# A shorter float64 decoding, and five blocks of w_out decoded piece by piece inside the first output tile

## The chip, the cores and the metric

One core of one Trainium2 chip runs the whole program. The metric is the device time of one execution in microseconds (us); lower is better. Five engines work side by side, each through its own list of instructions in order: PE (TensorE, matmuls), DVE (VectorE), ACT (ScalarE), POOL (GpSimd) and SP (SyncE), which here issues every DMA.

## The reference, cut to what matters

Three layers follow one another: a delta-rule attention over 768 steps (4 batches, 8 heads of 48), a soft mixture of experts over 32 slots ("slot MLP" below), and a two-layer MLP over all 3072 tokens. The last two are what the change touches:

```python
def _moe_ref(x, phi, w1, w2):
    ...
    for e in range(E):
        h = np.maximum(slot_input[e] @ w1[e], 0.0)
        slot_out[e] = h @ w2[e]
    ...
    return (c @ slot_out).astype(np.float32)

def _moe2_ref(x, w_in, w_out):
    h = x @ w_in                     # 3072x384 @ 384x2048
    g = np.maximum(0.01 * h, h)
    return (g @ w_out).astype(np.float32)   # 2048x384
```

`w_in` and `w_out` arrive as float64, all other arrays as float32.

## The kernel before, in words

**Stages.** Attention runs in 24 steps (`for s in range(NST)`, L658), each over 32 of the 768 positions, up to about 322 us. The slot MLP (L829 to L913) streams the 32 tiles of `w1` and `w2` (768 KB each, `load_w`, L556) through whatever SBUF slots are free and ends at about 377 us. The token MLP (L961 to L987) fills the rest: six tiles `B` of 512 tokens, each over 16 slices `ft` of the 2048 hidden features.

**The token MLP.** Since `x` is `c @ slot_out`, the kernel multiplies `slot_out` with `w_in` first: `make_G` (L924) computes 256 columns of that product with nine matmuls into one PSUM tile `gpsum`, ACT takes one part of it (`gh`, L935) and DVE writes `Gs` (L936). There are eight such sets, made during the first tile. For each slice: one matmul `hps` (L975), ACT copies it (`hs`, L980), DVE takes the maximum of h and 0.01 h (`gf`, L981), ACT rounds it to float16 (`gh`, L982), POOL forms the remainder (`gl`, L983). `down` (L938) then runs 12 matmuls into `ops` for the previous slice: eight with `gh`, four with `gl`. `hps` has two PSUM buffers, so the matmul of slice n+2 waits for the maximum of slice n. `gpsum` has one.

**Float64 decoding.** PE wants float16 pairs, so each 128x768 block of `w_in` and `w_out` (eight of each, 768 KB as float64) is decoded. `from_f64` (L508) works on the 32-bit words `hi` and `lo` with four DVE instructions: L513 and L514 build a float32 `top` from sign, exponent and upper mantissa of `hi`; L516 takes its power of two; L517 multiplies `lo` with that, which gives the rest `m`. Then ACT rounds 1024 `top` to float16 (L530 for `w_in`, L805 for `w_out`), and two more DVE instructions (L532 and L533, or L806 and L807) form the second float16. That is six DVE instructions and one ACT instruction per block.

**Where the blocks are decoded.** `w_in` blocks 0 to 4 are decoded during the last attention steps, 5 to 7 at the head of the slot MLP. `w_out` block q is loaded by `load_wo(q)` (L793, two buffers `raw64`) and decoded by `conv_wo(q)` (L798): blocks 0 to 3 inside the loop over the groups of the slot MLP (L889 to L896), blocks 4 to 7 at the slices 0 to 3 of the first token tile (L969 to L973), each as one piece. In the loop over groups `make_cT` (L814) also transposes the routing weights; DVE copies each transposed group from PSUM into `cT` (L825).

**What sets the order.** The text of the program does not fix an engine's list. The framework simulates a timeline and orders each engine by priority; `tc.high_priority` shifts a priority, `tc.issue_after(x)` keeps an instruction behind x. On the chip each list is then run strictly in order. A DMA list entry waits until the eighth DMA before it has landed, so SP has at most eight loads on their way, and an entry that waits for a buffer holds up all behind it.

Of the kernel before, what the change touches and what calls it, by code (L numbers as in the profile page):

```python
# [41 lines left out]
def drain(gen):  # L42
    for _ in gen:
        pass
# [3 lines left out]
def fused_kernel(ctx: ExitStack, tc: tile.TileContext, kq, kv, bu, phi, w1, w2, wi, wo, out):  # L48
# [458 lines left out]

    def from_f64(raw, m, top, scale):  # L508


        hi, lo = raw[:, :, 1], raw[:, :, 0]
        mf = m.bitcast(F32)
        ve.tensor_scalar(m, hi, 0x07FFFFFF, 3, ALU.bitwise_and, ALU.logical_shift_left)  # L513
        ve.scalar_tensor_tensor(top.bitcast(U32), hi, 0xC0000000, m, ALU.bitwise_and, ALU.bitwise_or)  # L514
        yield
        ve.tensor_scalar(m, top.bitcast(U32), 0xFF800000, None, ALU.bitwise_and)  # L516
        ve.scalar_tensor_tensor(mf, lo, scale, mf, MULT, MULT)  # L517
        yield
# [7 lines left out]
    def conv_wi(q):  # L526
        t = W[0, q] = place(3 * q, [128, 2, 768], F16)
        m, top = place(30, [128, 768], F32), place(33, [128, 768], F32)
        yield from from_f64(raw64.pop(q), m.bitcast(U32), top, 2.0 ** -42)
        sc.activation(t[:, 0], top, AF.Copy, scale=1024.0)  # L530
        yield
        ve.scalar_tensor_tensor(top, top, 1024.0, t[:, 0], MULT, SUB)  # L532
        ve.tensor_tensor(t[:, 1], top, m, ADD)  # L533
        yield
# [258 lines left out]
    def load_wo(q):  # L793
        raw = p_c.tile([128, 768, 2], U32, tag="raw64", name="raw64")
        sy.dma_start(raw.rearrange("p n w -> p (n w)"), wo[q].bitcast(U32))
        raw64[q] = raw

    def conv_wo(q):  # L798
        if q % 2 == 0:
            pair[0] = late([128, 2, 2, 768], F16, q // 2)  # L800
        t = W[1, q] = [pair[0][:, q % 2, i] for i in range(2)]
        m = p_c.tile([128, 768], U32, tag="m", name="m")
        top = p_c.tile([128, 768], F32, tag="top", name="top")
        drain(from_f64(raw64.pop(q), m, top, 2.0 ** -42))
        sc.activation(t[0], top, AF.Copy, scale=1024.0)  # L805
        ve.scalar_tensor_tensor(top, top, 1024.0, t[0], MULT, SUB)  # L806
        ve.tensor_tensor(t[1], top, m.bitcast(F32), ADD)  # L807

# [5 lines left out]
    def make_cT(g):  # L814
# [7 lines left out]
        for k in range(4):  # L822
            pe.transpose(tp[:, k, :], cs[:, k].rearrange("p a b c -> p (a b c)"), id16)

        ve.tensor_copy(cT[:, 512 * g:512 * g + 512].rearrange("p (k i b) -> p k b i", k=4, b=4),  # L825
                       tp.rearrange("p k (b i) -> p k b i", b=4))

# [40 lines left out]
    def convert(q):  # L868
        with tc.high_priority(offset=-500):
            conv_wo(q)  # L870

# [7 lines left out]
    for g in range(4):  # L879
# [9 lines left out]
        elif g < 3:  # L889
            if g == 1:  # L890
                free.extend([4, 5])
            convert(g - 1)
            load_wo(g + 1)
        else:
            convert(2)
            convert(3)  # L896
    with tc.high_priority(offset=CHAIN_PRIO):
# [40 lines left out]
    def down(B, ft, gh, gl, ops):  # L938
# [12 lines left out]
        for t in range(4):  # L951
# [7 lines left out]
            sy.dma_start(oT[4 * B + t], ob)  # L959

    Gs = p_os.tile([128, 2048], F16, name="Gs", bufs=1)  # L961
    with tc.high_priority(offset=CHAIN_PRIO):
        g_ins = make_G(0)
    for B in range(6):
        ops = [ps_o.tile([128, 384], F32, tag="o", name="ops") for _ in range(4)]
        for ft in range(16):
            if B == 0 and ft % 2 == 0 and ft < 14:
                make_G(ft // 2 + 1)
            if B == 0 and ft < 4:  # L969
                with tc.issue_after(last_w[0]):  # L970
                    load_wo(4 + ft)
                with tc.issue_after(g_ins):
                    convert(4 + ft)  # L973
            hps = ps_h.tile([128, 512], F32, tag="h", name="hps")
# [5 lines left out]
            sc.activation(hs, hps, AF.Copy, scale=2.0 ** -12)  # L980
            ve.scalar_tensor_tensor(gf, hps, 0.01 * 2.0 ** -12, hs, MULT, MAX)  # L981
            sc.activation(gh, gf, AF.Copy)  # L982
# [47 lines left out]
```

## Time and profile before

| what | us |
|---|---|
| median of 3 runs (lowest, highest) | 607.33 (603.05, 607.85) |
| the profiled execution, its own time | 609.56 |
| its span in the profile | 607.8 |
| DVE busy in the span | 410.2 |
| PE busy in the span | 515.0 |

The span is what the profiler saw from the first instruction to the last; 1.8 us of the execution lie around it. Views count from the start of the span. A row of a timeline that holds several instructions (x2) gives the time from the first start to the last end, so the distance between starts tells the pace better than the duration.

### The profile page before, as it was taken

How to read it: one execution, taken by the hardware profiler on the slowest of the kernel's cores; microseconds unless marked ns; L12 is line 12 of the kernel's file. 1: busy time of each engine (PE TensorE's matmuls, PEld its weight loads, DVE VectorE, ACT ScalarE, POOL GpSimd, SP SyncE). 2: the span in 40 equal slices, each digit the busy share in tenths (PEclk: the TensorE clock that was granted, in tenths of full speed). 3: DMA queues.
4: the chain of work that ended last, by engine and by line, in shares of the span. 5: the costliest groups of instructions: out<-in, count | busy, mean ns of one | idle time of the engine just before them, and what ended most of it. 6: DMA issues, size and time to landing. Idle time of an engine off the chain costs nothing.

```text
span 607.8 us, 20075 instructions
## 1 busy us (share of the span) xinstructions
PE 515.0 (85%) x8368; PEld 376.3 (62%) x8368; DVE 410.2 (67%) x1082; ACT 291.1 (48%) x696; POOL 207.6 (34%) x217
## 2 busy tenths in 40 slices
PE   7706888989989998976867677789999999999996
PEld 5605877978878988866752222456555555555553
DVE  3899988999779889997668966994424242333331
ACT  1313555546545666564432212545656565555552
POOL 9504212311331332431101000345554545454542
PEclk9655999999989999898966878999999999999999
DMA  9965775775966757769899996300101000010101
GB/s 237 252 131 108 150 173 123 171 192 102 215 139 139 170 121 191 181 177 252 209 398 416 415 414 249 104 1 2 52 1 53 0 29 25 2 53 1 53 0 53
DMA packets 71194, 87.37 MB, mean 144 GB/s; under 512 B 42944, under 2 KB 59584, under 8 KB 71104
## 3 DMA queue, kind: packets, MB, share of 16 engines
q1 hardware_dynamic: 71104, 86.09, 50.9%
q8 instruction: 66, 1.08, 0.8%
q14 instruction: 24, 0.20, 0.1%
HBM read 70.53 MB, written 4.72 MB: 124 GB/s over the span
## 4 chain that ended last, share of the span: by engine, by line
PE 61%; DVE 19%; DMA 11%; issue 4%; ACT 3%; SPq 1%; DVEq 0%; ACTq 0%
PE ops L943 28%; PE gm L189 6%; DMA arena<-in_w_dram 6%; PE sps L420 6%; PE hps L975 3%; PE ksu L377 3%; PE y L430 3%; PE ksu L369 2%; PE ksu L399 2%; DVE arena L283 2%; DMA kqb<-in_kq_dram 2%; PE y L385 2%; DVE arena L269 1%; DVE arena L287 1%; DVE arena L229 1%
## 5 line engine op out<-in xcount | busy, mean ns | idle before, releaser
L983 POOL TENSOR_TENSOR gl<-gf,gh 128x512 f16<-128x512 f32 x96 | 112.6, 1189 | 162.2 <-ACT gh L982 90.0
L943 PE MATMUL ops<-late,gh 128*128 128x384 f16 x768 | 143.6, 326 | 0.3 <-ACT gh L982 0.3
L981 DVE SCALAR_TENSOR_TENSOR gf<-hps,hs 128x512 f32<-128x512 f32 x96 | 62.3, 686 | 112.8 <-ACT hs L980 107.8
L943 PEld LDWEIGHTS <-gh 128*128 128x128 f16 x768 | 75.0, 98 | 56.7 <-ACT gh L982 3.0
L943 PE MATMUL ops<-late,gl 128*128 128x384 f16 x384 | 81.2, 326 | 0.2 <-POOL gl L983 0.2
L980 ACT ACTIVATE hs<-hps 128x512 f32<-128x512 f32 x96 | 52.5, 594 | 52.4 <-PE hps L975 52.4
L982 ACT ACTIVATE gh<-gf 128x512 f16<-128x512 f32 x96 | 60.4, 630 | 32.9 <-DVE gf L981 27.6
L327 POOL TENSOR_TENSOR vs<-kv,nn 128x384 f32<-128x384 f32 x24 | 20.4, 849 | 137.0 <-DMA kv<-in_kv_dram 90.1
L420 PE MATMUL sps<-u,khb 128*128 128x48 f16 x1104 | 55.0, 195 | 8.8 <-ACT u L404 2.8
L189 PE MATMUL gm<-kqr,arena 128*64 128x64 f32 x640 | 46.0, 311 | 18.6 <-DVE mm L205 18.6
L420 PEld LDWEIGHTS <-khb 128*128 128x128 f16 x1104 | 51.3, 117 | 13.9 <-issue 10.1
L283 DVE TENSOR_TENSOR arena<-arena 128x81 f32<-128x81 f32 (+12 forms) x150 | 55.4, 369 | 0.1
L189 PEld LDWEIGHTS gm<-kqr,arena 128*64 128x64 f32 x640 | 42.4, 222 | 20.7 <-DVE mm L205 18.9
L943 PEld LDWEIGHTS <-gl 128*128 128x128 f16 x384 | 37.4, 98 | 25.2 <-POOL gl L983 0.8
L269 DVE SCALAR_TENSOR_TENSOR arena<-arena 128x28 f32<-128x28 f32 (+27 forms) x186 | 51.9, 289 | 0.3
L287 DVE TENSOR_TENSOR arena<-arena 128x81 f32<-128x81 f32 (+12 forms) x150 | 51.1, 341 | 0.0
L399 PE MATMUL ksu<-z,tmb 128*128 128x48 f16 x576 | 27.4, 194 | 12.9 <-DMA tmb<-tc 5.5
L404 ACT ACTIVATE u<-ksu 128x192 f16<-128x192 f32 x48 | 15.7, 329 | 44.9 <-PE ksu L399 41.7
L430 PE MATMUL y<-u,tmb 128*128 128x48 f16 x576 | 35.2, 196 | 1.3 <-issue 1.3
L385 PE MATMUL y<-st,kqb 128*32 128x48 f32 x1472 | 29.2, 230 | 5.9 <-issue 5.9
L377 PE MATMUL ksu<-st,kqb 128*32 128x48 f32 x1472 | 33.1, 233 | 1.3 <-issue 0.7
L399 PEld LDWEIGHTS <-tmb 128*128 128x128 f16 x576 | 24.3, 118 | 15.8 <-issue 12.1
(167 smaller groups left out, 888.0 us busy)
## 6 DMA issues: line engine op xcount, KB each, us to landing
we<-in_w_dram SPq DMA_DIRECT2D x22, 768.0 KB, 12.4
kv<-in_kv_dram SPq DMA_DIRECT2D x24, 384.0 KB, 4.8
kqb<-in_kq_dram SPq DMA_DIRECT2D x46, 192.0 KB, 5.2
kqr<-in_kq_dram SPq DMA_DIRECT2D x20, 384.0 KB, 6.5
arena<-in_w_dram SPq DMA_DIRECT2D x10, 768.0 KB, 10.8
tmb<-tc SPq DMA_DIRECT2D x96, 64.0 KB, 3.4
arena<-in_wi_dram SPq DMA_DIRECT2D x8, 768.0 KB, 8.2
raw<-in_wo_dram SPq DMA_DIRECT2D x8, 768.0 KB, 14.1
```

The costliest lines, as they stand in the source:

```text
L189: end["gm"] = pe.matmul(gm[64 * bp:64 * bp + 64, h, :], kb[:, k, bp, :, h], c[:, k, bp, :, :, h], start=(h == 0), stop=True, skip_group_ch ...
L269: ve.scalar_tensor_tensor(R[:, i, 0:j], R[:, j, 0:j], gu[:, i, j:j + 1], R[:, i, 0:j], MULT, ADD)
L283: ve.tensor_tensor(tv, gu[:, j + 2:, j:j + 1].to_broadcast([128, n, w]), R[:, j:j + 1, 0:w].to_broadcast([128, n, w]), MULT)
L287: ve.tensor_tensor(R[:, j + 2:, 0:w], R[:, j + 2:, 0:w], tv, ADD)
L399: last_u[A] = pe.matmul(ksu[A][:, 256 + 48 * hh:304 + 48 * hh], tmb[s % 2][:, a, A, :, hh], z[:, b, 48 * hh:48 * hh + 48], start=False, st ...
L420: last_s[0] = pe.matmul(sps[A][:, bp, hh, :], kb[:, a, A, bp, :, hh], u[:, b, hh, :], start=False, stop=(s == NST - 2 and i == 2), skip_gr ...
L430: end["mu"] = pe.matmul(y[:, 4 * A + hh, :], mv[:, a, A, :, hh], u[:, b, hh, :], start=(s == 0 and A == 0 and hh == 0 and i == 0), stop=(i ...
L943: pe.matmul(ops[t], g[:, 128 * t:128 * t + 128], w, start=(ft == 0 and i == 0), stop=(ft == 15 and i == 2))
L980: sc.activation(hs, hps, AF.Copy, scale=2.0 ** -12)
L981: ve.scalar_tensor_tensor(gf, hps, 0.01 * 2.0 ** -12, hs, MULT, MAX)
L982: sc.activation(gh, gf, AF.Copy)
L983: gp.tensor_tensor(gl, gf, gh, SUB)
```

## The change

The decoding drops the rest `m`: a third DVE instruction shifts `lo` right by 29 bits and puts its three upper bits under the mantissa of `top`. The second float16 comes from `top` alone. That is four DVE instructions per block (new L510, L511, L513 and L528 or L800), and the float32 it passes through is the float64 cut at 23 mantissa bits. The two blocks of `w_in` in flight no longer share one `top`. `raw64` gets a third buffer. The copy into `cT` goes from DVE to ACT (new L819). Block 3 of `w_out` leaves the slot MLP; blocks 3 to 7 become a generator, `late_wo`, of three pieces each, and each slice of the first tile draws one piece (the first slice two) behind its maximum. Blocks 4 and 5 are requested right behind the last `w2` tile, 6 and 7 when the buffers of 3 and 4 have been read.

```diff
-    def from_f64(raw, m, top, scale):
-        hi, lo = raw[:, :, 1], raw[:, :, 0]
-        mf = m.bitcast(F32)
-        ve.tensor_scalar(m, hi, 0x07FFFFFF, 3, ALU.bitwise_and, ALU.logical_shift_left)
-        ve.scalar_tensor_tensor(top.bitcast(U32), hi, 0xC0000000, m, ALU.bitwise_and, ALU.bitwise_or)
-        yield
-        ve.tensor_scalar(m, top.bitcast(U32), 0xFF800000, None, ALU.bitwise_and)
-        ve.scalar_tensor_tensor(mf, lo, scale, mf, MULT, MULT)
+    def from_f64(raw, t):
+        hi, lo, t = raw[:, :, 1], raw[:, :, 0], t.bitcast(U32)
+        ve.tensor_scalar(t, hi, 0x07FFFFFF, 3, ALU.bitwise_and, ALU.logical_shift_left)
+        ve.scalar_tensor_tensor(t, hi, 0xC0000000, t, ALU.bitwise_and, ALU.bitwise_or)
+        yield
+        ve.scalar_tensor_tensor(t, lo, 29, t, ALU.logical_shift_right, ALU.bitwise_or)
         yield
...
     def conv_wi(q):
...
-        m, top = place(30, [128, 768], F32), place(33, [128, 768], F32)
-        yield from from_f64(raw64.pop(q), m.bitcast(U32), top, 2.0 ** -42)
+        top = place(33 if q % 2 else 30, [128, 768], F32)
+        yield from from_f64(raw64.pop(q), top)
         sc.activation(t[:, 0], top, AF.Copy, scale=1024.0)
         yield
-        ve.scalar_tensor_tensor(top, top, 1024.0, t[:, 0], MULT, SUB)
-        ve.tensor_tensor(t[:, 1], top, m, ADD)
+        ve.scalar_tensor_tensor(t[:, 1], top, 1024.0, t[:, 0], MULT, SUB)
         yield
...
-        raw = p_c.tile([128, 768, 2], U32, tag="raw64", name="raw64")
+        raw = p_c.tile([128, 768, 2], U32, tag="raw64", name="raw64", bufs=3)
...
-        m = p_c.tile([128, 768], U32, tag="m", name="m")
         top = p_c.tile([128, 768], F32, tag="top", name="top")
-        drain(from_f64(raw64.pop(q), m, top, 2.0 ** -42))
+        yield from from_f64(raw64.pop(q), top)
         sc.activation(t[0], top, AF.Copy, scale=1024.0)
-        ve.scalar_tensor_tensor(top, top, 1024.0, t[0], MULT, SUB)
-        ve.tensor_tensor(t[1], top, m.bitcast(F32), ADD)
+        ve.scalar_tensor_tensor(t[1], top, 1024.0, t[0], MULT, SUB)
+        yield
...
-        ve.tensor_copy(cT[:, 512 * g:512 * g + 512].rearrange("p (k i b) -> p k b i", k=4, b=4),
-                       tp.rearrange("p k (b i) -> p k b i", b=4))
+        sc.activation(cT[:, 512 * g:512 * g + 512].rearrange("p (k i b) -> p k b i", k=4, b=4),
+                      tp.rearrange("p k (b i) -> p k b i", b=4), AF.Copy)
...
             convert(2)
-            convert(3)
...
+    def late_wo():
+        for q in range(3, 8):
+            c = conv_wo(q)
+            next(c)
+            yield
+            next(c)
+            if q < 5:
+                with tc.issue_after(last_w[0]):
+                    load_wo(q + 3)
+            yield
+            next(c)
+            yield
+
+    with tc.issue_after(last_w[0]):
+        load_wo(4)
+        load_wo(5)
+    decode = late_wo()
...
-            if B == 0 and ft < 4:
-                with tc.issue_after(last_w[0]):
-                    load_wo(4 + ft)
-                with tc.issue_after(g_ins):
-                    convert(4 + ft)
...
-            ve.scalar_tensor_tensor(gf, hps, 0.01 * 2.0 ** -12, hs, MULT, MAX)
+            gf_ins = ve.scalar_tensor_tensor(gf, hps, 0.01 * 2.0 ** -12, hs, MULT, MAX).ins
+            if B == 0:
+                with tc.issue_after(gf_ins):
+                    for _ in range(1 if ft else 2):
+                        next(decode, None)
```

DVE at the head of the first token tile, before: `raw_7681` and `raw_7703` are blocks 4 and 5 of `w_out`.

```order
L936 SCALAR_TENSOR_TENSOR Gs<-gpsum,gh 128x256
L513 TENSOR_SCALAR m<-raw_7681 128x768
L513 TENSOR_SCALAR m<-raw_7703 128x768
L514 SCALAR_TENSOR_TENSOR top<-raw_7681,m 128x768
L514 SCALAR_TENSOR_TENSOR top<-raw_7703,m 128x768
L936 SCALAR_TENSOR_TENSOR Gs<-gpsum,gh 128x256
L516 TENSOR_SCALAR m<-top 128x768
L981 SCALAR_TENSOR_TENSOR gf<-hps,hs 128x512 x2
L516 TENSOR_SCALAR m<-top 128x768
L517 SCALAR_TENSOR_TENSOR m<-raw_7681,m 128x768
L806 SCALAR_TENSOR_TENSOR top<-top,late 128x768
L936 SCALAR_TENSOR_TENSOR Gs<-gpsum,gh 128x256
```

The same place in the changed kernel, where `raw_7514` and `raw_7616` are blocks 3 and 4 (L929 is the old L936, L986 the old L981):

```order
L929 SCALAR_TENSOR_TENSOR Gs<-gpsum,gh 128x256 x2
L986 SCALAR_TENSOR_TENSOR gf<-hps,hs 128x512
L510 TENSOR_SCALAR top<-raw_7514 128x768
L986 SCALAR_TENSOR_TENSOR gf<-hps,hs 128x512
L511 SCALAR_TENSOR_TENSOR top<-raw_7514,top 128x768
L929 SCALAR_TENSOR_TENSOR Gs<-gpsum,gh 128x256
L986 SCALAR_TENSOR_TENSOR gf<-hps,hs 128x512
L510 TENSOR_SCALAR top<-raw_7616 128x768
L513 SCALAR_TENSOR_TENSOR top<-raw_7514,top 128x768
L986 SCALAR_TENSOR_TENSOR gf<-hps,hs 128x512
L511 SCALAR_TENSOR_TENSOR top<-raw_7616,top 128x768
```

Four decoding instructions no longer stand between the first two `Gs`, and between two maxima stand at most three instructions of 768 columns and one `Gs`.

SP from the first `w_out` block to the last, before: `raw_7375` to `raw_7783` are blocks 0 to 7, `in_w_dram` holds `w1` and `w2`.

```order
L795 DMA raw_7375<-in_wo_dram 128x1536
L795 DMA raw_7377<-in_wo_dram 128x1536
L523 DMA arena<-in_wi_dram 128x1536
L562 DMA arena<-in_w_dram 128x1536 x3
L562 DMA we<-in_w_dram 128x1536 x9
L795 DMA raw_7472<-in_wo_dram 128x1536
L795 DMA raw_7536<-in_wo_dram 128x1536
L562 DMA arena<-in_w_dram 128x1536 x4
L795 DMA raw_7681<-in_wo_dram 128x1536
```

In the changed kernel (`raw_7361`, `raw_7363`, `raw_7453`, `raw_7514`, `raw_7616` are blocks 0 to 4):

```order
L790 DMA raw_7361<-in_wo_dram 128x1536
L790 DMA raw_7363<-in_wo_dram 128x1536
L790 DMA raw_7453<-in_wo_dram 128x1536
L519 DMA arena<-in_wi_dram 128x1536
L557 DMA arena<-in_w_dram 128x1536 x3
L557 DMA we<-in_w_dram 128x1536 x9
L790 DMA raw_7514<-in_wo_dram 128x1536
L557 DMA arena<-in_w_dram 128x1536 x4
L790 DMA raw_7616<-in_wo_dram 128x1536
```

Block 2 has moved ahead of one block of `w_in` and twelve tiles of `w1` and `w2`; the last four of these still stand behind four blocks of `w_out`.

DVE in attention step 21, before (`z` and `u` are small operands of PE, the L513 is block 2 of `w_in`):

```order
L393 SCALAR_TENSOR_TENSOR z<-ksu_157,z 128x192
L461 TENSOR_REDUCE mx_62<-lt 32x1
L393 SCALAR_TENSOR_TENSOR z<-ksu_158,z 128x192
L513 TENSOR_SCALAR arena<-arena 128x768
L500 TENSOR_REDUCE cm<-ce 128x4
```

and in the changed kernel:

```order
L510 TENSOR_SCALAR arena<-arena 128x768
L393 SCALAR_TENSOR_TENSOR z<-ksu_157,z 128x192
L461 TENSOR_REDUCE mx_62<-lt 32x1
L500 TENSOR_REDUCE cm<-ce 128x4
L511 SCALAR_TENSOR_TENSOR arena<-arena 128x768
L393 SCALAR_TENSOR_TENSOR z<-ksu_158,z 128x192
```

The decoding of the block, which waits for its load, now stands ahead of both `z` of the step.

## Rows read from the trace of the kernel before

**Rows 1.** Windows: window, length, busy us of PE, PEld, DVE, ACT, POOL; clock, DMA, GB/s.

```profile
330.00:340.00 10.00, 9.27 (x89) 4.28 (x90) 9.90 (x18) 3.12 (x9) 0.00 (x0) 1.00 1.02 417
...
360.00:370.00 10.00, 6.68 (x49) 2.70 (x42) 6.02 (x10) 1.97 (x3) 0.00 (x0) 0.99 1.01 411
...
380.00:390.00 10.00, 7.44 (x50) 4.73 (x50) 10.00 (x15) 5.36 (x10) 3.14 (x2) 1.00 0.21 60
```

**Rows 2.** The chain that ended last, 357 to 375 us: start, us, what.

```profile
357.79 13.69 DMA arena<-in_w_dram
...
371.53 3.54 PE son L862 x26
```

**Rows 3.** Timeline of PE, first token tile: start, us, line, operation.

```profile
377.82 1.15 PE L930 MATMUL gpsum<-arena,so 128*128 128x256 f16 x9
380.06 1.14 PE L930 MATMUL gpsum<-arena,so 128*128 128x256 f16 x9 [1.10 <-DVE Gs L936]
381.04 0.59 PE L975 MATMUL hps<-cT,Gs 128*128 128x512 f16 x2
...
384.95 1.46 PE L943 MATMUL ops<-late,gh 128*128 128x384 f16 x8
...
397.61 0.59 PE L975 MATMUL hps<-cT,Gs 128*128 128x512 f16 x2
398.04 1.46 PE L943 MATMUL ops<-late,gh 128*128 128x384 f16 x8
...
399.99 1.46 PE L943 MATMUL ops<-late,gh 128*128 128x384 f16 x8
...
420.78 0.38 PE L975 MATMUL hps<-cT,Gs 128*128 128x512 f16 x1
```

**Rows 4.** Timeline of DVE, same place.

```profile
379.59 0.42 DVE L936 SCALAR_TENSOR_TENSOR Gs<-gpsum,gh 128x256 f16<-128x256 f32 x1 [1.67 <-ACT gh L935]
379.93 1.02 DVE L513 TENSOR_SCALAR m<-raw 128x768 uint32<-128x768 uint32 x2
380.86 1.82 DVE L514 SCALAR_TENSOR_TENSOR top<-raw,m 128x768 uint32<-128x768 uint32 x2
382.60 0.42 DVE L936 SCALAR_TENSOR_TENSOR Gs<-gpsum,gh 128x256 f16<-128x256 f32 x1
...
383.40 1.28 DVE L981 SCALAR_TENSOR_TENSOR gf<-hps,hs 128x512 f32<-128x512 f32 x2
```

**Rows 5.** Timeline of ACT, same place.

```profile
382.57 1.59 ACT L805 ACTIVATE late<-top 128x768 f16<-128x768 f32 x2
```

**Rows 6.** Groups by form on DVE, 330 to 360 us: busy us, mean ns.

```profile
L825 DVE COPY cT<-tp 128x512 f16<-128x512 f16 x5 | 6.5, 1302 | 0.0
...
L514 DVE SCALAR_TENSOR_TENSOR top<-raw,m 128x768 uint32<-128x768 uint32 x2 | 1.9, 950 | 0.0
```

**Rows 7.** Groups by form on DVE, 380 to 412 us.

```profile
L514 DVE SCALAR_TENSOR_TENSOR top<-raw,m 128x768 uint32<-128x768 uint32 x4 | 5.6, 1430 | 0.0
...
L807 DVE TENSOR_TENSOR late<-top,m 128x768 f16<-128x768 f32 x4 | 4.7, 1184 | 0.0
L513 DVE TENSOR_SCALAR m<-raw 128x768 uint32<-128x768 uint32 x4 | 2.7, 706 | 0.0
```

**Rows 8.** Groups by form on POOL, 380 to 412 us.

```profile
L983 POOL TENSOR_TENSOR gl<-gf,gh 128x512 f16<-128x512 f32 x9 | 13.7, 1526 | 74.8 <-ACT gh L982 74.4 <-PE ops L943 0.4
```

**Rows 9.** Timeline of SP's queue, 345 to 356 us.

```profile
346.87 4.30 SPq L795 DMA_DIRECT2D raw<-in_wo_dram  x2
```

**Rows 10.** Timeline of DVE in attention step 21.

```profile
283.01 0.35 DVE L393 SCALAR_TENSOR_TENSOR z<-ksu,z 128x192 f16<-128x192 f32 x1
...
285.79 0.56 DVE L513 TENSOR_SCALAR arena<-arena 128x768 uint32<-128x768 uint32 x1 [1.34 <-DMA arena<-in_wi_dram]
```

**Rows 11.** Timeline of DVE in attention step 23.

```profile
303.71 0.36 DVE L393 SCALAR_TENSOR_TENSOR z<-ksu,z 128x192 f16<-128x192 f32 x1 [2.53 <-ACT z L392]
...
307.67 0.35 DVE L393 SCALAR_TENSOR_TENSOR z<-ksu,z 128x192 f16<-128x192 f32 x1
```

More of the change, by code (lines that the diff above doesn't have):

```diff
@@ L869, in convert @@
         with tc.high_priority(offset=-500):
-            conv_wo(q)
+            drain(conv_wo(q))
     def warm(n, ins):
```

## The prediction

> **What bounds the kernel now.** I read the windows first, then the chain of waits that ended last, then the timelines of PE, DVE and ACT where DVE is full. The windows show three regimes. While the slot MLP streams its weights the 16 DMA engines are full: 417 GB/s from 330 to 340 us and 411 from 360 to 370 [rows 1]; the windows between read the same. At the head of the token MLP DMA is nearly idle, DVE is busy for all of its 10.00 us and PE for only 7.44 of 10 [rows 1]. From some 420 us on PE is full to the end. So DVE time is worth something in one place alone, between 377 and 420 us. Before it, the chain shows the end of the slot MLP hanging on a load: 13.69 us from issue to landing at 371.5, then 26 matmuls [rows 2].
>
> How much PE loses behind that point I count in work, not in idle time. A set of nine `gpsum` matmuls takes 0.98 us (380.06 to 381.04), an `hps` 0.215 (two in 397.61 to 398.04), a round of twelve `ops` 1.95 (398.04 to 399.99) [rows 3]. Between 377.82 and 420.78 PE runs 8 sets, 14 `hps` and 12 rounds: 7.84 + 3.01 + 23.40 = 34.25 us of work in 42.96 us. So 8.7 us are lost, and only these are to be had. Of them 3.3 fall before the first `ops` at 384.95 (7.13 us, with 3 sets and 4 `hps`, 3.8 us, done) and 5.4 after it.
>
> **The change part by part.** *The head of the tile.* Today the second `Gs` waits behind four decoding instructions on DVE, from 379.93 to 382.60, and the first maximum starts at 383.40 [rows 4]; then ACT has two roundings of `w_out` (382.57, 1.59 us) ahead of its `gh` [rows 5], so `ops` starts at 384.95. In the new list both `Gs` come first. The second can run when its sum is rounded, near 381.7, the first maximum near 382.2, `gh` follows at once, since the first `w_out` rounding needs two more DVE pieces, and `ops` starts near 383.7. With 3 sets and 3 `hps` done (3.6 us) that loses 5.9 - 3.6 = 2.3 us, against 3.3: a gain of 1.0.
>
> *The stalls after it.* The work on DVE hardly falls: before, four blocks of six instructions, now five blocks of four. What changes is the place. PE needs one maximum per slice; today up to six decoding instructions separate two pairs of them, afterwards two or three. Whether DVE keeps up is a sum over slices 0 to 13, in which all 15 pieces fall. A two-input instruction of 768 columns takes 0.95 us in the slot MLP [rows 6], but 1.18 to 1.43 at the head of the tile [rows 7]; I take 1.31, the middle, and 0.71 for the one-input instruction. Two of a kind start closer than they last (1.82 us for two of 0.95 [rows 4]), so 0.08 comes off each: five blocks of 0.63 + 3 x 1.23 are 21.6 us. Fourteen maxima of 0.64 (1.28 for two [rows 4]) are 9.0, seven `Gs` of 0.42 are 2.9. DVE: 33.5 us. PE over the same slices: 14 x (1.95 + 0.215) + 7 x 0.98 = 37.2. DVE is then loaded to 90%, and PE sets the pace. I followed the first seven slices by hand with these durations and found each `gh`, `gl` and `Gs` ready before PE came to it. For the short waits that such a sum does not see I allow 1.0 us; at best it is 0. So 5.4 falls to 1.0.
>
> The new instruction, a shift with an or on two inputs, is in no row. Its bounds are the one-input shift (0.71 [rows 7]) and the slowest two-input form (1.43); I take the two-input mean, since it reads two tensors as L514 does. Five blocks times 0.7 us would change DVE's 33.5 by 3 us at most, which stays under 37.2.
>
> *The longer instructions.* They are longer exactly where POOL works beside them. Per `gl` of POOL, nine in 380 to 412 us [rows 8], four blocks lost about 16 x 0.36 + 8 x 0.15 = 7.0 us, 0.78 each. If the loss belongs to each `gl` rather than to each decoding instruction, 14 of them cost 10.9 instead of the 6.2 in my 33.5, DVE needs 38.2, and PE waits 1.0: that is the allowance.
>
> The Trainium skill, page "SBUF — State Buffer", section "Who interferes with whom", says that a DVE instruction with two SBUF inputs contends with a GpSimd instruction that reads SBUF, and that the second to issue "fully blocks" until the first ends. The rows agree that both slow down, but 0.78 per `gl` of 1.53 us [rows 8] is half a full block. By the rule a `gl` would always cost a whole one; that is the first rival.
>
> *Decoding in attention and slot MLP.* Eleven blocks, 0 to 7 of `w_in` and 0 to 2 of `w_out`, lose a one-input and a two-input instruction each (0.51 us, half of 1.02 [rows 4], and 0.95), block 3 leaves, and six copies of 1.30 us [rows 6] go to ACT. DVE gains some 28 us there. I count nothing for it: the last `w2` tile lands when DMA has moved all bytes ahead of it, and those are the same 32 tiles, eight blocks of `w_in` and four of `w_out` as before, in a queue that was full throughout. Cover gone would mean that SP holds a load back until the queue runs dry. Block 2 of `w_out` now goes ahead of twelve tiles, which come 1.9 us later (768 KB at the 414 GB/s of rows 1), the last four not. ACT has room for its copies: 3.12 us busy in the 10 us that hold most of the roundings [rows 1]. Against the change speaks one place: in step 21 the decoding of `w_in` block 2, which got its data at 285.79, now stands ahead of a `z` that ran at 283.01 [rows 10]. That `z` comes about 3.3 us late, PE somewhat less; the queue covers it. In step 23 the opposite happens: a `z` that stood behind a decoding until 307.67, while its twin ran at 303.71 [rows 11], is now ahead. For the end of the slot MLP I bound both together by -2 and +1 us, and take 0.
>
> *Sum.* -1.0 - 4.4 = -5.4 us. The profiled execution took 609.56 us, so such a one would take 604.2. The three runs have a median of 607.33, 2.2 us lower; from it, 601.9.
>
> **The rivals.** *A full block at the port.* If the interleaved decoding meets a `gl` each time and one of the two waits it out, 14 `gl` cost 14 x 1.53 = 21.4 us, DVE needs 27.3 + 21.4 = 48.7 against PE's 37.2, and PE loses 11.5 on top of the 2.3: 13.8 instead of 8.7, 612.4 us, slower than before. It decides from 1.2 us per `gl` on, where PE's loss reaches 8.7. For it: DVE and POOL now overlap in every slice, where before DVE had long stretches without a `gl`. Against it: 0.78 measured in the same place. Between 0.8 and 1.2 us per `gl` lies a gain of 5 to 0, about 604.8 in the middle.
>
> *The shorter attention comes through.* If the last weight lands earlier because DVE frees buffers and steps sooner, up to 3 us (of the 4.0 between the two `z` [rows 11]) add to the gain: 598.9. Against it: DMA is full while the weights stream [rows 1]. For it: the `z` that comes earlier stands before that stretch, and nothing here shows DMA full there.
>
> *SP held at block 3.* The load of block 3 of `w_out` takes over the buffer of block 0, whose third decoding instruction must have read it, and the last four tiles stand behind it on SP. Before, such a load went at 346.87 [rows 9], and the queue held 13.7 us of work. If DVE, now in order behind two groups' copies in the slot MLP, reads block 0 after some 360 us, the queue runs dry; at 368 the last tile would land about 8 us late, 609.9 us in all. The point where nothing is left of the gain is near 365. I expect the read near 341, so this is the least likely.
>
> **How the numbers follow.** The forecast 0.68, with a range of its own from 600 to 604; the half-way block at the port 0.13, the full one 0.05, the earlier landing 0.10, the held queue 0.04. Runs of this kernel alone lie 603.05 to 607.85, so 1% (6.1 us) is about what a measurement can tell from no change. The range that leaves out 2 in 10 reaches from the earlier landing to the port: 598.0 to 606.0. Faster by over 1% is below 601.3: 0.35 of the forecast's chance and most of the earlier landing, 0.44; slower by over 1% holds part of the port and of the queue, 0.05; the rest is 0.51.
>
> **What would show each step.** Right: the last tile of `w2` lands at 371.5 +- 1.5; the first `ops` comes 5.9 us after the first `gpsum`; from there to the end of the first tile PE has few gaps behind DVE, and DVE is under 9.5 of 10 us; two-input decoding stays between 1.0 and 1.4 us. Wrong: DVE full for the whole of the first tile with PE below 8 of 10 (port); a DMA window below 350 GB/s between 330 and 370 us (queue); or the first `gpsum` several us from 377.8.

## The result, and the profile after

The changed kernel took 600.23 us, median of four runs (597.79 to 600.47), beside 606.52 for the kernel before, now from four runs too: a ratio of 0.9891, 95% interval 0.9849 to 0.9933. Three later sessions have the kernel before at 607.16, 607.77 and 606.12, and a second measurement of the change gave 601.85 and 0.9892 (0.9812 to 0.9971). Ratios leave disturbed runs out, as they do two of the four runs with six instructions in pieces below, so that a ratio can differ from the quotient of the two medians. The profiled execution took 600.38 us, its span is 598.7, 9.1 shorter than before. Where these 9.1 us arose can be read off five marks, the same in both traces: the last instruction of the last solve (L295 on DVE), the 26 matmuls on the last `w2` tile, the first `gpsum`, the first `ops`, the end.

| us | L295 starts | to the 26 matmuls | to the first gpsum | to the first ops | to the end | span |
|---|---|---|---|---|---|---|
| before | 266.13 | 105.40 | 6.29 | 7.13 | 222.85 | 607.8 |
| before, second profile (third experiment) | 263.22 | 105.49 | 7.11 | 7.14 | 222.54 | 605.5 |
| after | 264.27 | 105.16 | 5.51 | 5.84 | 217.92 | 598.7 |
| after, second profile | 266.07 | 106.96 | 5.52 | 5.83 | 217.92 | 602.3 |

From the first `gpsum` on the change wins 229.98 - 223.76 = 6.22 us (second profiles: 229.68 - 223.75 = 5.93), and these columns repeat to a few tenths. Between the 26 matmuls and the first `gpsum` it wins 0.78 (1.59). The first column is no effect: up to L295 both kernels hold the same instructions. The spans are printed to 0.1 us, so that a sum up to the end is good to some 0.05.

The windows of the changed kernel, which answer to [rows 1]:

```profile
330.00:340.00 10.00, 9.83 (x96) 3.70 (x88) 3.75 (x14) 6.09 (x11) 0.00 (x0) 1.00 1.01 410
360.00:370.00 10.00, 7.88 (x66) 3.31 (x63) 0.29 (x2) 0.60 (x1) 0.00 (x0) 1.00 1.01 411
380.00:390.00 10.00, 9.94 (x65) 6.08 (x63) 10.00 (x14) 5.79 (x11) 5.81 (x4) 1.00 0.24 79
390.00:400.00 10.00, 10.00 (x68) 6.32 (x66) 9.52 (x13) 6.46 (x13) 5.06 (x4) 1.00 0.21 80
```

The weight stream is as full as before, with DVE down from 9.90 to 3.75 us in the first window: what was freed there is idle time. In the token tile DVE is still busy for all of 10 us, and PE now for 9.94 instead of 7.44: a full engine that PE hardly waits for. The chain that ended last still goes through the last load and its 26 matmuls [rows 2]:

```profile
356.46 12.93 DMA arena<-in_w_dram
369.38 0.04 issue
369.43 2.77 PE son L856 x26
```

The timeline of PE [rows 3]; the first `ops` at 380.78, and then one operation behind the other:

```profile
374.94 1.15 PE L923 MATMUL gpsum<-arena,so 128*128 128x256 f16 x9
377.19 1.14 PE L923 MATMUL gpsum<-arena,so 128*128 128x256 f16 x9 [1.10 <-DVE Gs L929]
378.17 0.59 PE L980 MATMUL hps<-cT,Gs 128*128 128x512 f16 x2
...
380.78 1.47 PE L936 MATMUL ops<-late,gh 128*128 128x384 f16 x8
382.09 0.38 PE L980 MATMUL hps<-cT,Gs 128*128 128x512 f16 x1
382.30 0.81 PE L936 MATMUL ops<-late,gl 128*128 128x384 f16 x4
382.95 1.46 PE L936 MATMUL ops<-late,gh 128*128 128x384 f16 x8
384.25 1.15 PE L923 MATMUL gpsum<-arena,so 128*128 128x256 f16 x9
```

The timeline of DVE [rows 4]. Both `Gs` and both first maxima (L986) stand ahead of the first long decoding instruction (L511):

```profile
376.71 0.42 DVE L929 SCALAR_TENSOR_TENSOR Gs<-gpsum,gh 128x256 f16<-128x256 f32 x1 [1.67 <-ACT gh L928]
378.88 0.42 DVE L929 SCALAR_TENSOR_TENSOR Gs<-gpsum,gh 128x256 f16<-128x256 f32 x1 [1.74 <-ACT gh L928]
379.37 0.69 DVE L986 SCALAR_TENSOR_TENSOR gf<-hps,hs 128x512 f32<-128x512 f32 x1
379.97 0.55 DVE L510 TENSOR_SCALAR top<-raw 128x768 uint32<-128x768 uint32 x1
380.44 0.68 DVE L986 SCALAR_TENSOR_TENSOR gf<-hps,hs 128x512 f32<-128x512 f32 x1
381.04 1.73 DVE L511 SCALAR_TENSOR_TENSOR top<-raw,top 128x768 uint32<-128x768 uint32 x1
...
386.84 1.90 DVE L800 SCALAR_TENSOR_TENSOR late<-top,late 128x768 f16<-128x768 f32 x1
388.67 0.94 DVE L513 SCALAR_TENSOR_TENSOR top<-raw,top 128x768 uint32<-128x768 uint32 x1
...
390.52 0.96 DVE L800 SCALAR_TENSOR_TENSOR late<-top,late 128x768 f16<-128x768 f32 x1
```

The groups by form on DVE, 378 to 412 us [rows 7]; L513 is the new shift with an or:

```profile
L511 DVE SCALAR_TENSOR_TENSOR top<-raw,top 128x768 uint32<-128x768 uint32 x5 | 7.6, 1527 | 0.1
L800 DVE SCALAR_TENSOR_TENSOR late<-top,late 128x768 f16<-128x768 f32 x4 | 4.8, 1192 | 0.3 <-ACT late L799 0.3
L513 DVE SCALAR_TENSOR_TENSOR top<-raw,top 128x768 uint32<-128x768 uint32 x5 | 4.7, 945 | 0.0
L510 DVE TENSOR_SCALAR top<-raw 128x768 uint32<-128x768 uint32 x5 | 3.8, 752 | 0.0
```

A block is 1.53 + 1.19 + 0.95 + 0.75 = 4.42 us, a third of it per slice 1.47. With a maximum of 0.68 and half a `Gs` of 0.42 a slice asks 2.36 us of DVE, where PE has 1.95 + 0.215 + 0.49 = 2.65 to do: 89%. (The fifth L800 stands behind 412 us and takes 0.96; with it the block is 4.37 us and the load the same.) The idle time ahead of L510 is 0.0, so no block waits for its load there, and the earlier requests and the third buffer are not what limits the tile.

### The profile page after: what moved, and what is told of

Same layout as the page of the kernel before. It is cut to its first block, busy times and chain, and to the rows that moved or that the text cites. A ratio compares the mean times of both kernels' runs of the same rounds, so it can differ in the third digit from the quotient of the medians.

```text
span 598.7 us, 20034 instructions
## 1 busy us (share of the span) xinstructions
PE 512.1 (86%) x8368; PEld 376.8 (63%) x8368; DVE 380.2 (64%) x1044; ACT 297.8 (50%) x702; POOL 205.4 (34%) x217
## 4 chain that ended last, share of the span: by engine, by line
PE 64%; DVE 16%; DMA 10%; ACT 4%; issue 3%; SPq 2%; POOL 0%; DVEq 0%; ACTq 0%
PE ops L936 31%; PE gm L189 6%; PE sps L420 5%; DMA arena<-in_w_dram 4%; PE hps L980 3%; DMA we<-in_w_dram 3%; PE ksu L377 2%; PE ksu L369 2%; PE y L430 2%; DVE arena L269 2%; PE ksu L399 2%; DVE arena L283 2%; DVE arena L287 2%; DVE arena L229 2%; PE y L385 1%
## 5 line engine op out<-in xcount | busy, mean ns | idle before, releaser
L936 PE MATMUL ops<-late,gh 128*128 128x384 f16 x768 | 143.6, 326 | 0.1
L986 DVE SCALAR_TENSOR_TENSOR gf<-hps,hs 128x512 f32<-128x512 f32 x96 | 62.6, 686 | 109.8 <-ACT hs L985 109.3
L936 PEld LDWEIGHTS <-gh 128*128 128x128 f16 x768 | 74.8, 98 | 54.8 <-ACT gh L991 1.4
L936 PE MATMUL ops<-late,gl 128*128 128x384 f16 x384 | 81.2, 326 | 0.0
L936 PEld LDWEIGHTS <-gl 128*128 128x128 f16 x384 | 37.6, 98 | 25.0
L423 ACT ACTIVATE st<-sps 128x384 f32<-128x384 f32 x46 | 22.4, 492 | 24.9 <-PE sps L420 24.6
```

Source lines behind the costliest of these rows:

```text
L936: pe.matmul(ops[t], g[:, 128 * t:128 * t + 128], w, start=(ft == 0 and i == 0), stop=(ft == 15 and i == 2))
L986: gf_ins = ve.scalar_tensor_tensor(gf, hps, 0.01 * 2.0 ** -12, hs, MULT, MAX).ins
```

## The experiments

**Is it the place of the decoding, or the number of its instructions?** Two kernels have one of the two each; their edits, like all below, are cut to the lines that matter. *Four instructions in the old place:*

```
+            convert(3)
...
+            if B == 0 and ft < 4:
+                with tc.issue_after(last_w[0]):
+                    load_wo(4 + ft)
+                with tc.issue_after(g_ins):
+                    convert(4 + ft)
...
-                with tc.issue_after(gf_ins):
-                    for _ in range(1 if ft else 2):
-                        next(decode, None)
```

> The change without its third part: w_out decoded by four instructions, but block 3 whole in the slot MLP and blocks 4 to 7 whole in the first four slices, as before the change. Theory P (the gain comes from where the decoding stands: pieces behind the maxima instead of whole blocks ahead of the early slices): VectorE's whole blocks of now about 3.8 us each still stand ahead of slices 0 to 3 against 2.65 us of TensorE's work per slice, so of the 6.2 us that the changed kernel wins from the first gpsum on (229.98 before, 223.76 after) at least a third is lost again: 226 to 228 from the first gpsum to the end of the span, median about 603. Rival C (it comes from fewer instructions of decoding, wherever they stand): 224.5 or less, median within 1 us of the changed kernel's 600.2.

Median 602.16 of ten runs, ratio 0.9928 (0.9892 to 0.9964); from the first `gpsum` to the end 228.00 us. As theory P has it: of the 6.2 us 4.2 are lost again, 2.05 of them ahead of the first `ops` (7.89 instead of 5.84) and 2.19 behind it. The timeline of DVE shows the picture of [rows 4] again: the same four instructions between the first two `Gs`, which start 3.01 us apart in both:

```profile
371.28 0.42 DVE L930 SCALAR_TENSOR_TENSOR Gs<-gpsum,gh 128x256 f16<-128x256 f32 x1 [1.67 <-ACT gh L929]
371.62 1.02 DVE L510 TENSOR_SCALAR top<-raw 128x768 uint32<-128x768 uint32 x2
372.55 1.82 DVE L511 SCALAR_TENSOR_TENSOR top<-raw,top 128x768 uint32<-128x768 uint32 x2
374.29 0.42 DVE L930 SCALAR_TENSOR_TENSOR Gs<-gpsum,gh 128x256 f16<-128x256 f32 x1
```

The head is even 0.76 longer than before (7.13), and all that this kernel wins from the first `gpsum` on arises behind the first `ops`: 220.11 us, 2.74 less than before.

*Six instructions in the new place* (the old `from_f64` as `from_f64_six`, for `w_out` alone):

```
-        yield from from_f64(raw64.pop(q), top)
+        m = p_c.tile([128, 768], U32, tag="m", name="m")
+        yield from from_f64_six(raw64.pop(q), m, top, 2.0 ** -42)
...
+            convert(3)
...
-        for q in range(3, 8):
+        for q in range(4, 8):
...
+        load_wo(6)
```

> The changed kernel with w_out's decoding back at six instructions of VectorE, blocks 4 to 7 by pieces behind the maxima, block 3 in the slot MLP (w_in stays at four, the copies of cT stay on ScalarE). Theory P: pieces of two instructions (about 1.4 to 2.1 us) and a maximum of 0.68 and a fifth of a microsecond of Gs make 2.3 to 2.9 us per slice beside TensorE's 2.65, so that little or nothing is lost behind the first ops: 224 to 227 from the first gpsum to the end of the span, median 600 to 603. Rival C: the whole gain goes, 229 to 230, median about 606.

Median 605.36 of four runs (596.92 to 607.55), ratio 0.9898 (0.9823 to 0.9972); from the first `gpsum` to the end 228.67. Here theory P fell: the head is as after the change (5.82), but 222.85 us remain behind the first `ops`, 4.93 more than after. I had reckoned with durations that a `gl` beside them does not stretch. The groups by form on DVE in the first token tile, 368.5 to 402.5 us:

```profile
L520 DVE SCALAR_TENSOR_TENSOR top<-raw,m 128x768 uint32<-128x768 uint32 x4 | 6.7, 1680 | 0.0
L811 DVE SCALAR_TENSOR_TENSOR top<-top,late 128x768 f32<-128x768 f32 x4 | 5.7, 1431 | 0.0
L523 DVE SCALAR_TENSOR_TENSOR m<-raw,m 128x768 f32<-128x768 uint32 x4 | 5.7, 1416 | 0.0
...
L812 DVE TENSOR_TENSOR late<-top,m 128x768 f16<-128x768 f32 x3 | 2.8, 944 | 0.0
L519 DVE TENSOR_SCALAR m<-raw 128x768 uint32<-128x768 uint32 x4 | 2.2, 554 | 0.0
```

With another one-input instruction of 0.55 (L522) a block is 6.57 us, 2.19 per piece, 3.08 per slice: 0.43 more than PE's 2.65. Four blocks are 12 pieces, 12 x 0.43 = 5.2 us, and 4.93 were lost. (The fourth L812, behind 402.5 us, takes 1.81; with it the block is 6.79 and the sum 6.0, so that it gives the size and no more.) So neither the place nor the number is the cause by itself. Either alone wins 1.3 to 2.0 us, both together 6.2. The place decides the head: 7.13 and 7.89 us with whole blocks, 5.84 and 5.82 with pieces. Behind the first `ops` six instructions take 222.85 us in either place and four take 220.11 and 217.92: there the place helps only once a slice fits.

**Is it DVE's sum per slice?** Without POOL's `gl` in the first tile the instructions shrink while their number stays. The edit, on the changed kernel and on the one with six instructions in pieces:

```
-            gp.tensor_tensor(gl, gf, gh, SUB)
-            pend.append((B, ft, gh, gl, ops))
+            if B:
+                gp.tensor_tensor(gl, gf, gh, SUB)
+            pend.append((B, ft, gh, gl if B else gh, ops))
```

> The changed kernel without POOL's remainder gl in the first token tile (the third product takes gh in its place there, so the remainder's share of the output's first tile is left out; the matmuls are as many). Theory: POOL's gl and VectorE's two-input instructions hold each other up, so that the decoding instruction L511, 1527 ns with gl beside it, falls to 0.9 to 1.05 us. As VectorE is no longer what the tile waits for, the time from the first gpsum to the end of the span stays at 223.8 within 0.5. Rival: the first tile is still bound by VectorE somewhere, and the time falls by more than 0.5; or the duration stays at 1.3 to 1.5 us, and it isn't POOL that makes it long.

> Six instructions in pieces, as in the run before, now without POOL's remainder gl in the first token tile (its share of the output's first tile is left out). Theory: what a slice asks of VectorE decides. With gl a six-instruction block took .55 + 1.68 + .55 + 1.42 + 1.43 + .94 = 6.57 us, 2.19 per piece, with a maximum of .68 and .21 of Gs 3.08 per slice against TensorE's 2.65, and the tile lost 4.9 us more than with four instructions. Without gl the block is 4 x .95 + 2 x .55 or less, 4.6 to 4.9 us, 2.4 to 2.5 per slice, below 2.65: so 223.5 to 224.5 from the first gpsum to the end of the span. Rival (it is the number of instructions or the place of a deadline, not VectorE's sum): 227 or more.

From the first `gpsum` to the end 223.51 us with four instructions, 223.54 with six: six instructions in pieces cost nothing in the tile when no `gl` stretches them. The groups by form on DVE of the first of the two:

```profile
L511 DVE SCALAR_TENSOR_TENSOR top<-raw,top 128x768 uint32<-128x768 uint32 x5 | 4.8, 953 | 0.1
L800 DVE SCALAR_TENSOR_TENSOR late<-top,late 128x768 f16<-128x768 f32 x5 | 4.8, 952 | 0.0
L513 DVE SCALAR_TENSOR_TENSOR top<-raw,top 128x768 uint32<-128x768 uint32 x5 | 4.8, 951 | 0.0
...
L510 DVE TENSOR_SCALAR top<-raw 128x768 uint32<-128x768 uint32 x5 | 2.7, 549 | 0.0
```

A four-instruction block is 3.40 us alone and 4.42 beside `gl`; a six-instruction one 4.90 (4 x 0.95 + 2 x 0.55) and 6.57. With a maximum and half a `Gs` the first three are 2.02, 2.36 and 2.52 us per slice, below PE's 2.65, and the last is 3.08, above it.

**Does what the change does ahead of the tile matter?** The change once more; the change with its attention parts undone; and each of these two parts undone by itself:

```
-        top = place(33 if q % 2 else 30, [128, 768], F32)
-        yield from from_f64(raw64.pop(q), top)
+        m, top = place(30, [128, 768], F32), place(33, [128, 768], F32)
+        yield from from_f64_six(raw64.pop(q), m.bitcast(U32), top, 2.0 ** -42)
...
-        sc.activation(cT[:, 512 * g:512 * g + 512].rearrange("p (k i b) -> p k b i", k=4, b=4),
-                      tp.rearrange("p k (b i) -> p k b i", b=4), AF.Copy)
+        ve.tensor_copy(cT[:, 512 * g:512 * g + 512].rearrange("p (k i b) -> p k b i", k=4, b=4),
+                       tp.rearrange("p k (b i) -> p k b i", b=4))
```

> The changed kernel once more, beside the kernel before on the chip of the other experiments. Theory: of the 9.2 us between the two profiled executions the 1.9 that arose up to the last instruction of the last solve (L295, at 266.13 before and 264.27 after) are scatter of a stretch whose instructions are the same. Up to that instruction this run comes out anywhere between 256 and 267 us, from there to the last w2 tile's matmuls at 105.2 within 0.3, from the first gpsum to the end of the span at 223.8 within 0.4; median 599 to 601. Rival (the change moves the earlier stretch too): L295 at 263 to 265 again.

> The changed kernel with all that it does outside w_out's decoding undone: w_in by six instructions of VectorE, and the copies of cT on VectorE. Theory (this freed VectorE for some 25 us where the DMA queue bounds, and is worth nothing): from L295 to the last w2 tile's matmuls 105.0 to 105.6 us, from the first gpsum to the end of the span 223.8 within 0.4. Rival (the shorter decoding in attention and slot MLP comes through): 1 to 3 us more from L295 to the last w2 tile's matmuls.

> The changed kernel with the copies of cT back on VectorE, w_in left at four instructions. The 26 matmuls on the last w2 tile took 3.54 us before, 2.77 in eight kernels with the change's slot MLP, and 4.31 with both parts of it undone, at a granted clock of .55 to .60, 1.00 and .50. Theory (TensorE's clock there hangs on the copies, which make TensorE's transposes wait and change what it did ahead of the gap at 343 to 356 us): 3.5 to 4.4 us here, 5.5 + .8 to 1.6 us from them to the first gpsum. Rival (it hangs on w_in's decoding, or on where the run happens to fall): 2.77 and 5.51. From the first gpsum to the end of the span 223.75 within 0.3 by either.

> The changed kernel with w_in decoded by six instructions, the copies of cT left on ScalarE. Theory (the clock hangs on the copies): the last 26 matmuls 2.77 us, 5.51 to the first gpsum. Rival (it hangs on w_in's decoding): 3.5 to 4.4 us. From L295 to the last w2 tile's matmuls 105 to 107 and from the first gpsum to the end 223.75 within 0.3 by either.

> The kernel before, profiled a second time. Theory: from the first gpsum to the end of the span 230.0 within 0.4, as in its first profile (229.98), whatever the time ahead of it; the last 26 matmuls 3.5 us or more again, if the clock hangs on the instructions, and 2.77 if it hangs on where the run falls; L295 anywhere from 256 to 267.

| us | L295 starts | to the 26 matmuls | these take | first gpsum to the end |
|---|---|---|---|---|
| the change again | 266.07 | 106.96 | 2.77 | 223.75 |
| both parts undone | 262.98 | 106.53 | 4.31 | 223.73 |
| copies of `cT` on VectorE | 260.41 | 102.93 | 2.77 | 223.74 |
| `w_in` by six | 261.75 | 106.38 | 2.77 | 223.75 |
| before again | 263.22 | 105.49 | 4.36 | 229.68 |

The last column shows that these parts do nothing in the token tile: 223.73 to 223.75 in all four. L295 came at 266.07, against the rival's 263 to 265: that part of the first difference is scatter, 255.86 to 266.13 over all runs. The way from L295 to the last tile scatters too: 105.16 and 106.96 in two runs of the same change, and 102.93 to 106.53 with one or both parts undone, so that this column decides nothing; my 0.3 was too narrow.

What I had not foreseen is the third column. The 26 matmuls are slow in both profiles of before (3.54 and 4.36) and with both parts undone, and take 2.77 in all eleven others, also with one part undone, so neither half of my theory on the copies holds. The timeline of PE, before again and with both parts undone:

```profile
368.71 4.36 PE L862 MATMUL son<-arena,hz 128*32 128x384 f32 x26 [0.35 <-DMA arena<-in_w_dram]
```

```profile
369.51 4.31 PE L867 MATMUL son<-arena,hz 128*32 128x384 f32 x26 [1.00 <-DMA arena<-in_w_dram]
```

The windows ahead of these matmuls and from their start, with both parts undone:

```profile
363.51:369.51 6.00, 2.87 (x14) 0.72 (x11) 0.29 (x2) 0.60 (x1) 0.00 (x0) 0.98 1.02 418
369.51:373.51 4.00, 4.00 (x26) 1.21 (x26) 0.00 (x0) 0.00 (x0) 0.00 (x0) 0.61 0.26 106
```

and in the changed kernel without `gl`, whose instructions up to there are those of the change:

```profile
361.37:367.37 6.00, 2.88 (x11) 0.83 (x10) 0.29 (x2) 0.60 (x1) 0.00 (x0) 1.00 1.02 416
367.37:371.37 4.00, 4.00 (x33) 1.58 (x34) 0.00 (x1) 0.49 (x1) 0.00 (x0) 1.00 0.49 200
```

The granted clock is at the lower level of 1.2 GHz for most of the four microseconds in the one (0.61 on the mean) and stays at 2.4 GHz in the other, after 2.87 and 2.88 us of PE's work in the six before. That undoing both parts brings the slow matmuls back, and undoing one does not, was seen once each; all three profiles without either part have the fall and no other has it. Why the clock falls stays open.

**A faster kernel.** DMA is full until the last `w2` tile lands and nearly idle after it, and DVE is all but idle from 359 to 373 us (0.29 us busy in the window from 360 to 370). So the loads of `w_out` blocks 2 and 3 can go behind the last tile, with block 2 decoded in DVE's idle time. Three versions differ in where the third piece of block 2 stands (L799 on ACT, then L800 on DVE):

```
-        for q in range(3, 8):
+        for q in range(2, 8):
...
     with tc.issue_after(last_w[0]):
+        load_wo(2)
+        load_wo(3)
         load_wo(4)
-        load_wo(5)
     decode = late_wo()
+    with tc.high_priority(offset=-500):
+        for _ in range(3):
+            next(decode)
```

> The changed kernel with the loads of w_out's blocks 2 and 3 moved from ahead of the last w2 tiles to behind the last one, and block 2 decoded by pieces too (its three ahead of slice 0, the other blocks' behind the maxima as before). Theory: from 330 to 370 us the DMA queue bounds, and 2 blocks of 786 KB at about 410 GB/s are 3.8 us, so the last w2 tile lands 3 to 4 us earlier and the first gpsum starts as much earlier, while VectorE's extra three instructions of some 3.5 us fit in its idle time ahead of the first gpsum (359 to 373 us): median 596 to 598. Rival: the slot MLP's own chain bounds as soon as the loads are earlier, or block 2's decoding ends late and delays Gs: 599.5 to 601.

```
-        for _ in range(3):
+        for _ in range(2):
```

> The kernel with blocks 2 and 3 loaded behind the last w2 tile, and now only two pieces of block 2 ahead of the first slice, its third behind the first maximum. Theory: in the run before the third piece (0.85 us of ScalarE, then VectorE) held the copies of so and with them the first gpsum by 0.6 and Gs by 0.8; without it the first ops stand 5.84 us behind the first gpsum (6.62 in the run before) and the rest is 223.8 from the first gpsum on (224.55); from L295 to the last w2 tile's matmuls 99.4 again; median 592 to 594. Rival: one more piece in the slices makes VectorE late by a slice, and the tile loses it again: 224.5 or more.

```
+        with tc.issue_after(a_ins), tc.issue_after(g_ins):
+            next(decode)
```

> The kernel with blocks 2 and 3 loaded behind the last w2 tile, two pieces of block 2 ahead of the first slice, and now its third between the first two columns of Gs, where VectorE stands idle for 1.7 us and ScalarE too; the slices have fifteen pieces again. Theory: the first ops stand 5.84 us behind the first gpsum, and from the first gpsum to the end of the span it is 223.8, as in the changed kernel (224.55 with the third piece ahead of so, 224.46 with it behind the first maximum); from L295 to the last w2 tile's matmuls 99 to 101; median 592 to 595. Rival: ScalarE's part of the third piece holds the second gh or the first hs, and the first ops come 6.2 us or more behind the first gpsum.

| third piece | median us | ratio, interval | L295 to the 26 matmuls | first gpsum to first ops | to the end |
|---|---|---|---|---|---|
| ahead of `so` | 593.91 | 0.9791 (0.9748 to 0.9833) | 99.39 | 6.62 | 217.93 |
| behind the first maximum | 596.14 | 0.9824 (0.9758 to 0.9890) | 100.71 | 5.95 | 218.51 |
| between the first two `Gs` | 592.96 | 0.9797 (0.9747 to 0.9846) | 100.91 | 5.84 | 217.90 |

All three beat before and, by their medians, the change; their intervals overlap, so they are not told apart by time. By the marks the last is what was meant: the 26 matmuls start 99.4 to 100.9 us behind L295 in all three, against 102.9 to 107.0 in the eleven profiles that load these blocks earlier, and the tile of the last is as in the changed kernel, 223.74 from the first `gpsum` on. In the first version ACT's part stood ahead of its `so`, as the timeline of ACT shows:

```profile
367.95 0.84 ACT L799 ACTIVATE late<-top 128x768 f16<-128x768 f32 x1 [1.08 <-DVE top L513]
368.70 0.69 ACT L902 ACTIVATE so<-ss 128x128 f16<-128x128 f32 x3
```

In the second the rival came true but for 0.04: 224.46 us, of which 0.6 are lost behind the first `ops`. The next piece met a `gl`, and the maximum that PE needed next stood behind it; first the timeline of POOL, then that of DVE:

```profile
374.91 1.16 POOL L994 TENSOR_TENSOR gl<-gf,gh 128x512 f16<-128x512 f32 x1 [54.63 <-ACT gh L993]
```

```profile
374.95 1.53 DVE L510 TENSOR_SCALAR top<-raw 128x768 uint32<-128x768 uint32 x1
376.40 0.68 DVE L988 SCALAR_TENSOR_TENSOR gf<-hps,hs 128x512 f32<-128x512 f32 x1
```

In the third, the timeline of DVE has the piece in what was a gap:

```profile
369.03 0.42 DVE L927 SCALAR_TENSOR_TENSOR Gs<-gpsum,gh 128x256 f16<-128x256 f32 x1 [1.33 <-ACT gh L926]
369.76 0.96 DVE L800 SCALAR_TENSOR_TENSOR late<-top,late 128x768 f16<-128x768 f32 x1 [0.31 <-ACT late L799]
371.20 0.42 DVE L927 SCALAR_TENSOR_TENSOR Gs<-gpsum,gh 128x256 f16<-128x256 f32 x1 [0.47 <-ACT gh L926]
```

## Why the prediction was right

Forecast was 601.9 us, 5.4 below before; measured were 6.3 between the medians, 600.23. That the two lie so close is in part luck: by the marks the tile won 6.22 (5.93) and a clock that the sum did not have 0.78 (1.59), while the stretch up to L295 alone scatters by 10 us.

*What bounds.* Right: only the head of the token MLP pays. The 28 us of DVE's time freed ahead of it moved no mark in any run that could be told from scatter, but for the clock (below).

*The head.* Right. Forecast 5.9 us from the first `gpsum` to the first `ops`, measured 5.84, by the named route: both `Gs` first, `gh` at once.

*The stalls after it.* Right in mechanism, and its allowance of 1.0 us is the mis-sized term. The first `ops` to the end fell by 4.93 us, with 0.215 more for the `hps` that PE now has behind the first `ops`; of the 5.4 lost before 5.4 - 5.15 = 0.25 is left (0.56 with the second profiles' 4.62). The allowance was for short waits and for `gl`, and without `gl` the changed kernel gains 223.76 - 223.51 = 0.25. DVE's load was forecast at 33.5 us or 90%; the same 41 instructions (five blocks, 14 maxima, seven `Gs`) kept it busy for 31.99 us, 86% (the 89% above adds durations that overlap by some 0.08 each). What I did not see is how near the six-instruction form stood to the edge: I wrote that the work on DVE hardly falls and that the place changes. By the second experiment the place alone wins 1.3 us of the 6.2, so the sum was right and that sentence was not.

*The longer instructions.* The mean was right enough (1.31 us taken, 1.53, 1.19 and 0.95 measured, 1.22 in the middle), the reading of it was not. I took 0.78 us per `gl` for half a full block. One by one the rows show that the later instruction waits for all that is left of the earlier one. The `gl` of 386.55 in the timeline of POOL of the changed kernel ends at 387.93,

```profile
386.55 1.38 POOL L992 TENSOR_TENSOR gl<-gf,gh 128x512 f16<-128x512 f32 x1 [0.45 <-ACT gh L991]
```

and the L800 issued at 386.84 ends at 388.74: 0.96 before that is 387.78, about when the `gl` is through, while the L800 of 390.52, which meets none, takes 0.96. The Trainium skill ("SBUF — State Buffer", "Who interferes with whom") has the rule that the later one "fully blocks"; it says these words of DVE's two-port modes, and the rows agree for L800, which has two inputs in SBUF. It does not charge a whole `gl` each time, as the prediction read it and my rival reckoned: a blocked instruction pays only the rest of the running one, and many `gl` hold up none. By the means, five blocks lost 5 x (4.42 - 3.40) = 5.1 us beside 13 `gl`, 0.39 each. The maximum, which reads one input from PSUM, never grew (0.67 to 0.69).

*The end of the slot MLP.* Taken as 0 within -2 and +1. The landing held within the scatter: the 26 matmuls start 105.40 and 105.16 us behind L295 (105.49 and 106.96 in the second profiles), with 410 GB/s or more throughout. The 0.78 to 1.59 us at the 26 matmuls came from PE's clock, a term that the sum did not have. The feared `z` of step 21 came 18.14 us behind L295 instead of 16.88 (second profiles: 18.15 and 15.55), so 1.3 to 2.6 us late where 3.3 were forecast, and the mark at the 26 matmuls does not show it; the load of block 3 went at 346.69, as its kind did before [rows 9], so SP was not held.

*What would show it.* Four signs misled. DVE was to be under 9.5 of 10 us and reads 10.00 and 9.52. Blocked instructions count as busy, but that is not all: in the changed kernel without `gl` DVE is as full in the first of these windows and idle for much of the second, with PE at the same 9.94 and 10.00 (windows as far behind the first `gpsum` as the two from 380 us above). DVE works ahead there, so that its busy time says little of who waits:

```profile
377.95:387.95 10.00, 9.94 (x65) 6.08 (x63) 10.00 (x17) 7.40 (x14) 0.00 (x0) 1.00 0.39 141
387.95:397.95 10.00, 10.00 (x68) 6.46 (x66) 5.59 (x9) 5.52 (x10) 0.00 (x0) 1.00 0.05 18
```

Two-input decoding was to stay between 1.0 and 1.4 us; by lines it reads 1.53, 1.19 and 0.95, and singly 0.94 to 1.90. The last tile was to land at 371.5 +- 1.5 and landed at 369.38, with 1.9 us of scatter ahead of it, and the first `gpsum` came 2.9 us from the 377.8 whose distance was to be a sign against: such signs are better given from a mark nearby.

## What to carry to other kernels

Where one engine feeds another slice by slice, add up what a slice asks of each, with the durations as they are beside the neighbours of that place: here slices at 3.08 against 2.65 us lost some 5 us in all, and slices at 2.36 at most 0.6. Putting work behind the due operation and shortening it can each win little alone and much together. Place a mark just ahead of the stretch in question: here the time from it on repeated to 0.3 us in the two profiles of either kernel, while the mark itself scattered by 10.

## What was not expected of the hardware

DVE's decoding and POOL's `gl` take turns instruction by instruction, and even the one-input L510, 0.55 us alone, took 1.53 where a `gl` had begun 0.04 us before it. It goes the other way too: in the changed kernel a `gl` that begins inside an L513 (384.13 to 385.07) takes 1.65 us, where one that meets nothing takes 1.16, as the timeline of POOL shows:

```profile
384.45 1.65 POOL L992 TENSOR_TENSOR gl<-gf,gh 128x512 f16<-128x512 f32 x1 [0.66 <-ACT gh L991]
```

The granted clock of PE fell at the end of the slot MLP in three profiles and in eleven it did not, with the same 2.9 us of work in the six before in one of each kind, worth up to 1.6 us. And the stretch up to L295, with the same instructions in all fourteen profiles, ended anywhere from 255.86 to 266.13 us, the widest scatter of all the marks. The mean granted clock up to the mark goes with it in part (0.95 where the mark came first, 0.91 and 0.90 where it came last, but 0.90 also where it came at 261.75); what causes the scatter is open.
